# An attention-and-MLP kernel on one Trainium2 core: from blocks of 768 tokens per batch entry to blocks of 384 queries of all heads, each followed by its MLP block

## The chip, the cores and the metric

The kernel runs on one core of one Trainium2 chip. The metric is the device time of one execution in microseconds (us); the kernel before takes 378.56 us (median of three runs, 377.82 to 378.64). Every run has a state, fast or slow, given by its time against the fastest run of the same kernel (over 1.5% longer is slow). Engines are called PE (matrix multiply), PEld (its weight load), DVE (vector), ACT (activations), POOL and SP (here it mainly issues DMA transfers). The "span" of a profile runs from the first to the last instruction of one execution and is about 1.7 us shorter than the time.

## The reference, cut to what matters

q, k and v are [4 batches, 8 heads, 768 tokens, 64], in f32. For each query, an upper bound of its score is worked out for each chunk of 32 keys; the six best chunks that are not in the future are kept, the rest is masked; attention follows, and its output x (3072 tokens of 512 columns) goes through an MLP with an ELU between.

```python
k_min = np.min(k_chunks, axis=3); k_max = np.max(k_chunks, axis=3)
ub = np.sum(np.maximum(q * k_min, q * k_max), axis=-1)        # one bound per query and chunk
top_chunks = np.argsort(np.where(causal, ub, -1e9), axis=-1)[..., -6:]
mask = sel & (pos[:, None] >= pos[None, :])                   # chosen chunk and causal
attn = softmax(np.where(mask, scale * q @ k.T, -1e9))
x = (attn @ v).transpose(0, 2, 1, 3).reshape(B * S, H * D)
h = x @ w_in                                                  # 512 -> 2048
g = np.where(h > 0.0, h, np.exp(np.minimum(h, 0.0)) - 1.0)
return g @ w_out                                              # 2048 -> 512
```

## The kernel before

Two heads make a pair; four pairs make a batch entry, and 16 pairs make the whole. For each pair, `prep` transposes k and q on PE (`psK`, `psQ`, in the PSUM pool psT) and copies them out as bf16 operands of the scores (`lhs`, `rhs`). `select` computes the bounds (`ub`), finds the six best chunks, transposes the resulting mask and sends it by DMA into spare rows of `rhs`, where it enters the scores as extra rows of the contraction. `attend` computes scores (`sps`), exponentials (`pt`) and the attention output, and transposes it on PE into `xt`. `mlp` takes a batch entry and a half of its tokens: PE fills `h_ps`; ACT, POOL and DVE turn it into `gT`, which frees the `h_ps` buffer; PE then fills `o_ps`.

```python
psT = pool("psT", 2, space=bass.MemoryType.PSUM)   # psK, psQ, ub, pxt
psS = pool("psS", 2, space=bass.MemoryType.PSUM)   # sps
psO = pool("psO", 1, space=bass.MemoryType.PSUM)
psM = pool("psM", 3, space=bass.MemoryType.PSUM)   # h_ps, o_ps

    # select(g): the mask goes by one DVE transpose and four DMAs
    selT = selpool.tile([P, NQS], BF16, name="selT")
    nc.vector.transpose(out=selT, in_=sb[:, :, :].rearrange("p b c -> p (b c)"))
    for j in range(2):
        s = (2 * g + j) % NSET
        nc.sync.dma_start(out=rhsA[s][64:64 + NCH, Q0:S], in_=selT[64 * j:64 * j + NCH, :])
        nc.sync.dma_start(out=rhsB[s][0:NCH, Q0:S], in_=selT[64 * j + 32:64 * j + 32 + NCH, :])
    ...
    # mlp(b, hf): one of 16 columns of the hidden layer
    for kk in range(NKK):
        nc.tensor.matmul(hw, lhsT=w_in_sb[:, kk, P * fc:P * (fc + 1)],
                         rhs=xT[NPAIR * b + kk][:, ts], start=(kk == 0), stop=(kk == NKK - 1))
    nc.scalar.activation(out=e_sb, in_=hw, func=AF.Exp)
    nc.gpsimd.tensor_scalar(out=m_sb, in0=e_sb, scalar1=-1.0, scalar2=1.0, op0=AOT.add, op1=AOT.mult)
    nc.vector.scalar_tensor_tensor(out=gT[:, fc, :], in0=hw, scalar=0.0, in1=m_sb,
                                   op0=AOT.max, op1=AOT.min)
    ...
    # the order: attention of all pairs of a batch entry, MLP two groups of pairs later
    for g in range(ng):
        attend(2 * g)
        if g + 1 < ng: select(g + 1)
        attend(2 * g + 1)
        if g + 2 < ng: prep_group(g + 2)
        if g % 2 == 1 and g >= 3:
            for hf in range(2): mlp((g - 3) // 2, hf)
    for hf in range(2): mlp(B - 1, hf)
```

The pools have eight PSUM buffers in all: 2 psT, 2 psS, 1 psO, 3 psM. The program fixes the order of instructions on each engine, with the attention of one batch entry woven into the MLP of another.

The softmax here doesn't subtract the row's maximum and nothing guards it: scores larger than these inputs give would overflow.

Of the kernel before, what the change touches and what calls it, by code (L numbers as in the profile page):

```python
# [9 lines left out]
AOT = mybir.AluOpType  # L10
# [5 lines left out]
B = 4  # L16
# [11 lines left out]
HS = S // 2  # L28
NFC = DFF // P
# [5 lines left out]
NSET = 4  # L35
Q0 = TOPK * CHUNK
NQB = NCH - TOPK
NQS = S - Q0
HB = NQB // 2
HQ = HB * CHUNK  # L40


@with_exitstack
def kernel(
# [17 lines left out]
    smpool = pool("smpool", 3)  # L62
    selpool = pool("selpool", 2)
    ptpool = pool("ptpool", 10)
    opool = pool("opool", 3)
    xtpool = pool("xtpool", 10)
    gtpool = pool("gtpool", 2)
    mlppool = pool("mlppool", 4)
    psT = pool("psT", 2, space=bass.MemoryType.PSUM)
    psS = pool("psS", 2, space=bass.MemoryType.PSUM)  # L70
    psO = pool("psO", 1, space=bass.MemoryType.PSUM)
    psM = pool("psM", 3, space=bass.MemoryType.PSUM)

    npairs = B * NPAIR


    def load(t):
        b, r = divmod(t, NPAIR)
        k_pair = ldpool.tile([P, NQT, 2, D], F32, name="k_pair")
        q_pair = ldpool.tile([P, NQT, 2, D], F32, name="q_pair")  # L80
        for h in range(2):
            nc.sync.dma_start(out=k_pair[:, :, h, :],
                              in_=k[b, 2 * r + h].rearrange("(n p) d -> p n d", p=P))
        for h in range(2):
            nc.sync.dma_start(out=q_pair[:, :, h, :],
                              in_=q[b, 2 * r + h].rearrange("(n p) d -> p n d", p=P))
        return k_pair, q_pair

    def load_v(t):
        b, r = divmod(t, NPAIR)  # L90
        v_pair = ldpool.tile([P, NQT, 2, D], F32, name="v_pair")
        for h in range(2):
            nc.sync.dma_start(out=v_pair[:, :, h, :],
                              in_=v[b, 2 * r + h].rearrange("(n p) d -> p n d", p=P))
        return v_pair

    lds = {t: load(t) for t in range(2)}
    ldv = {t: load_v(t) for t in range(2)}
# [6 lines left out]
    ident_b = const.tile([P, P], BF16, name="ident_b")  # L105
    nc.vector.tensor_copy(out=ident_b, in_=ident_f)

    vexts, lhsA, lhsB, rhsA, rhsB, kst = [], [], [], [], [], []
    for s in range(NSET):
        vexts.append(const.tile([P, NQT, 2, D + 1], BF16, name=f"vext{s}"))  # L110
        lhsA.append(const.tile([P, S], BF16, name=f"lhsA{s}"))
        lhsB.append(const.tile([P, S], BF16, name=f"lhsB{s}"))
        rhsA.append(const.tile([P, S], BF16, name=f"rhsA{s}"))
        rhsB.append(const.tile([P, S], BF16, name=f"rhsB{s}"))
        kst.append(const.tile([P, 2, 64], F32, name=f"kst{s}"))

    def cast_v(t):
        return nc.gpsimd.tensor_scalar(out=vexts[t % NSET][:, :, :, 0:D], in0=ldv.pop(t), scalar1=1.0,
                                       scalar2=0.0, op0=AOT.mult, op1=AOT.add)

    for s in range(NSET):
        nc.vector.memset(kst[s], 0.0)
        nc.vector.memset(vexts[s][:, :, :, D:D + 1], 1.0)
        nc.vector.memset(rhsA[s][64:P, :], 0.0)
        nc.vector.memset(rhsB[s][0:64, :], 0.0)

    econst = const.tile([P, NCH, CHUNK], BF16, name="econst")
    nc.vector.memset(econst, MASKNEG)
    for r0 in (0, 64):
        nc.gpsimd.affine_select(out=econst[r0:r0 + 64], in_=econst[r0:r0 + 64],  # L130
                                compare_op=AOT.is_equal, fill=0.0, base=0,
                                pattern=[[1, NCH], [0, CHUNK]], channel_multiplier=-1)
    for s in range(NSET):
        nc.vector.tensor_copy(out=lhsA[s][64:P, :],
                              in_=econst[64:P].rearrange("p c w -> p (c w)"))
        nc.vector.tensor_copy(out=lhsB[s][0:64, :],
                              in_=econst[0:64].rearrange("p c w -> p (c w)"))

# [4 lines left out]
    selb = [const.tile([P, NQB, CHUNK], BF16, name=f"selb{i}") for i in range(2)]  # L143
    for i in range(2):
        nc.gpsimd.memset(selb[i], 0.0)
# [3 lines left out]

# [8 lines left out]


    qf = {}  # L160

    def prep(t):
        s = t % NSET
        k_pair, q_pair = lds.pop(t)
        kmm = smpool.tile([P, 2, NCH], F32, name="kmm")
        for h in range(2):
            ps = psT.tile([P, HS], F32, name="psK", tag="ps")
            for n in range(3):
                nc.tensor.transpose(ps[:, P * n:P * (n + 1)], k_pair[:, 3 * h + n], ident_f)  # L169
            pv = ps[:, :].rearrange("p (c w) -> p c w", w=CHUNK)  # L170
            cs = slice(12 * h, 12 * h + 12)
            nc.vector.tensor_reduce(out=kmm[:, 0, cs], in_=pv, axis=AX.X, op=AOT.min)  # L172
            nc.vector.tensor_reduce(out=kmm[:, 1, cs], in_=pv, axis=AX.X, op=AOT.max)  # L173
            ts = slice(HS * h, HS * (h + 1))
            nc.scalar.activation(out=lhsA[s][0:64, ts], in_=ps[0:64, :], func=AF.Copy)
            nc.scalar.activation(out=lhsB[s][64:P, ts], in_=ps[64:P, :], func=AF.Copy)  # L176
        for h in range(2):
            rows = slice(64 * h, 64 * h + 64)
            cols = slice(32 * h, 32 * h + NCH)
            nc.gpsimd.tensor_copy(out=kst[s][rows, 0, cols], in_=kmm[rows, 0, :])  # L180
            nc.gpsimd.tensor_tensor(out=kst[s][rows, 1, cols], in0=kmm[rows, 1, :],
                                    in1=kmm[rows, 0, :], op=AOT.subtract)
        QTf = qfpool.tile([P, NQS], F32, name="QTf")
        Qrl = qfpool.tile([P, NQS], F32, name="Qrl")
        qf[t] = (QTf, Qrl)
        for h in range(2):
            ps = psT.tile([P, HS], F32, name="psQ", tag="ps")
            for n in range(3):
                nc.tensor.transpose(ps[:, P * n:P * (n + 1)], q_pair[:, 3 * h + n], ident_f)  # L189
            ts = slice(HS * h, HS * (h + 1))  # L190
            if h == 0:
                nc.scalar.activation(out=QTf[:, 0:HS - Q0], in_=ps[:, Q0:HS], func=AF.Copy)
            else:
                nc.scalar.activation(out=QTf[:, HS - Q0:], in_=ps, func=AF.Copy)  # L194
            nc.scalar.activation(out=rhsA[s][0:64, ts], in_=ps[0:64, :], func=AF.Copy)
            nc.scalar.activation(out=rhsB[s][64:P, ts], in_=ps[64:P, :], func=AF.Copy)  # L196
        nc.vector.tensor_scalar(out=Qrl, in0=QTf, scalar1=0.0, scalar2=None, op0=AOT.max)  # L197


    def select(g):  # L200
        ubT = selpool.tile([P, NQB, CHUNK], F32, name="ubT")
        for u in range(2):
            ub = psT.tile([P, HQ], F32, name="ub", tag="ps")
            for w in range(2):
                for j in range(2):
                    t = 2 * g + j
                    nc.tensor.matmul(ub[64 * j:64 * j + 64, :], lhsT=kst[t % NSET][:, w, :],  # L207
                                     rhs=qf[t][w][:, HQ * u:HQ * (u + 1)],
                                     start=(w == 0), stop=(w == 1))
            nc.vector.transpose(out=ubT[:, HB * u:HB * (u + 1), :].rearrange("p b c -> p (b c)"),  # L210
                                in_=ub)
        nc.vector.memset(ubT[:, 0, TOPK + 1:TOPK + 2], -BIG)
        thr8 = selpool.tile([P, NQB, 8], F32, name="thr8")
        for bb in range(NQB):
            nc.vector.max(out=thr8[:, bb, :], in_=ubT[:, bb, 0:max(8, bb + TOPK + 1)])
        sb = selb[g % 2]
        nc.vector.tensor_tensor(out=sb[:, :, 0:NCH], in0=ubT[:, :, 0:NCH],
                                in1=thr8[:, :, TOPK - 1:TOPK].to_broadcast([P, NQB, NCH]),
                                op=AOT.is_lt)
        selT = selpool.tile([P, NQS], BF16, name="selT")  # L220
        nc.vector.transpose(out=selT, in_=sb[:, :, :].rearrange("p b c -> p (b c)"))
        for j in range(2):
            s = (2 * g + j) % NSET
            nc.sync.dma_start(out=rhsA[s][64:64 + NCH, Q0:S], in_=selT[64 * j:64 * j + NCH, :])
            nc.sync.dma_start(out=rhsB[s][0:NCH, Q0:S], in_=selT[64 * j + 32:64 * j + 32 + NCH, :])
# [6 lines left out]

    def attend(t):
        s = t % NSET
        lhs = (lhsA[s], lhsB[s])
        rhs = (rhsA[s], rhsB[s])
        xt = xtpool.tile([P, S], BF16, name="xt")
        xT[t] = xt
        for grp in range(2):
            seg = {}  # L240
            for segs in steps[grp]:
# [3 lines left out]
                for hd in range(2):  # L245
                    if not (both and hd == 1):
                        sps = psS.tile([P, 512], F32, name="sps")
# [142 lines left out]
```

## Time and profile before

| stage of the profiled run | length, us | PE busy, us | PE clock | DMA share |
|---|---|---|---|---|
| start, loads and first heads | 36 | 17.7 | 0.89 | 0.88 |
| heads, no MLP result yet | 49 | 38.5 | 0.73 | 0.97 |
| attention and MLP mixed | 205 | 186.0 | 0.98 | 0.22 |
| MLP alone | 88.3 | 76.5 | 1.00 | 0.09 |

The table is the view by windows of the kernel before, whose rows follow. Its columns are the window, its length, busy time of each engine (with the number of instructions), then the granted PE clock as a share of full speed, the busy share of the DMA engines, and GB/s.

```profile
core 0: us, PE busy (x) PEld busy (x) DVE busy (x) ACT busy (x) POOL busy (x), PEclk, DMA share, GB/s
0.00:36.00 36.00, 17.71 (x65) 10.55 (x66) 20.67 (x68) 17.02 (x37) 12.67 (x35) 0.89 0.88 183
36.00:85.00 49.00, 38.47 (x301) 21.85 (x300) 24.55 (x92) 34.20 (x72) 8.81 (x17) 0.73 0.97 186
85.00:290.00 205.00, 186.01 (x1487) 106.04 (x1495) 125.11 (x371) 147.46 (x329) 56.15 (x127) 0.98 0.22 57
290.00:378.30 88.30, 76.53 (x412) 38.17 (x414) 34.98 (x64) 26.75 (x54) 25.70 (x50) 1.00 0.09 37
```

Busy time of PE is not work: at half clock an instruction is busy for longer and does the same. In one run three transposes of k take 0.90 us at clock 0.50 and 0.49 at full clock. So the page's engine line and its slices are read together. One caution: in this trace the view by windows gives a clock of 1.00 for the first 24 us, yet three transposes of q take 0.90 us there (at 13.14 us), so the 0.89 of the first stage says too much. The slices cut the span into 40 parts of 9.5 us; a digit is tenths busy (9 is 90% or more), and the clock is in tenths of full speed.

```profile
PE 318.7 (84%) x2260; PEld 176.6 (47%) x2272; DVE 205.3 (54%) x594; ACT 225.4 (60%) x489; POOL 103.3 (27%) x228
...
PE   1476876889599999599997799999999989979886
...
PEclk9995697589989999989998999999999999999999
DMA  9949999935914526501000000102000100101002
```

PE is busy 84% of the time, but the fourth to the ninth digit of its clock line (28 to 85 us) lie between 5 and 9 tenths, and the DMA line stands at 9 in seven of the first eight slices. The view of waits (who waited, for what; us in total, times, longest) has PE's largest total wait, which lies within the MLP:

```profile
PE h_ps L302 <- DVE gT L310: 12.8, 24, 2.4
```

The timeline of ACT, kernel before, gives the moment of the first MLP result, when the first `h_ps` is evicted (read out of its buffer). Columns: start, length, engine and line, instruction with its count, and in brackets the idle time just before it with what ended it.

```profile
85.56 1.25 ACT L306 ACTIVATE e_sb<-h_ps 128x384 f32<-128x384 f32 x3
```

The same kind of view, the timeline, of PE in the kernel before shows the tail:

```profile
328.69 2.11 PE L302 MATMUL h_ps<-xt,w_in_sb 128*128 128x384 bf16 x12 [0.53 <-DVE gT L310]
331.32 2.12 PE L302 MATMUL h_ps<-xt,w_in_sb 128*128 128x384 bf16 x12 [0.52 <-DVE gT L310]
```

The first `h_ps` is evicted (read out of its buffer) at 85.56 us, since an MLP block waits for four whole pairs. PE's first MLP matmul is much earlier, as the view of the tile `h_ps` up to 90 us shows (count, shortest/median/longest in ns, first and last start):

```profile
L302 PE MATMUL h_ps<-xt,w_in_sb x19: 323/325/527, 43.5 to 89.8; 128*128 128x384 bf16 x19
```

It starts at 43.5 us with the first pair's share of the sum and then waits for the other pairs.

In the tail, three `h_ps` buffers let 12 matmuls pass (2.11 us), then PE stands for 0.52 us until `gT` frees one.

Two lines from the chain that ended last (start, length, what) show what holds the first heads: a load of k, and a mask on its way by DMA.

```profile
36.67 9.29 DMA k_pair<-in_k_dram
...
53.91 4.36 DMA rhsA_137<-selT
```

### The profile page before, as it was taken

To read this page: it belongs to the slowest core of one execution; us is meant where nothing else is said; L and a number is where in the kernel's file an instruction comes from. 1 tells how busy PE (TensorE), PEld (TensorE's weight loads), DVE (VectorE), ACT (ScalarE), POOL (GpSimd) and SP (SyncE) were. 2 spreads that over 40 slices of the span, in tenths; PEclk is the share of its full clock that TensorE was granted. 3 is DMA by queue.
4 is the path that set the end of the run, shared out by engine and by line. 5 is a ranking of instruction groups with operands and counts; after the bars stand their busy time and mean duration, and the time that the engine had idled before them with its cause. 6 is when DMAs were issued, how large, how long until landed. Compare 5 with 4: busy or idle time off the path is not lost.

```text
span 378.3 us, 6504 instructions
## 1 busy us (share of the span) xinstructions
PE 318.7 (84%) x2260; PEld 176.6 (47%) x2272; DVE 205.3 (54%) x594; ACT 225.4 (60%) x489; POOL 103.3 (27%) x228
## 2 busy tenths in 40 slices
PE   1476876889599999599997799999999989979886
PEld 1333444455265455354564454545556444444442
DVE  7553275367477475561694683651867154261540
ACT  1638757858968965950879758653797052350430
POOL 4414022003133112340331231430123053250430
PEclk9995697589989999989998999999999999999999
DMA  9949999935914526501000000102000100101002
GB/s 205 277 74 192 203 181 177 280 71 118 209 42 98 125 71 161 117 2 55 30 12 2 1 14 28 58 0 83 5 11 2 57 29 26 58 3 55 28 2 83
DMA packets 84129, 30.67 MB, mean 81 GB/s; under 512 B 76160, under 2 KB 81024, under 8 KB 84096
## 3 DMA queue, kind: packets, MB, share of 16 engines
q1 hardware_dynamic: 79872, 26.06, 27.7%
q0 software_dynamic: 4224, 4.19, 7.1%
q8 instruction: 18, 0.29, 0.3%
q14 instruction: 15, 0.12, 0.1%
HBM read 27.26 MB, written 6.29 MB: 89 GB/s over the span
## 4 chain that ended last, share of the span: by engine, by line
PE 27%; issue 23%; ACT 21%; POOL 12%; DVE 11%; DMA 4%; POOLq 0%; SPq 0%; ACTq 0%; DVEq 0%
POOL m_sb L308 12%; PE o_ps L315 8%; ACT pt L253 6%; PE sps L250 4%; PE ub L207 4%; PE h_ps L302 4%; DMA k_pair<-in_k_dram 2%; DVE gT L310 2%; PE psQ L189 2%; ACT e_sb L306 2%; ACT QTf L194 1%; PE psK L169 1%; DMA rhsA_137<-selT 1%; ACT pt L256 1%; PE pxt L291 1%
## 5 line engine op out<-in xcount | busy, mean ns | idle before, releaser
L302 PE MATMUL h_ps<-xt,w_in_sb 128*128 128x384 bf16 x512 | 108.4, 333 | 13.2 <-DVE gT L310 12.8
L308 POOL TENSOR_SCALAR m_sb<-e_sb 128x384 f32<-128x384 f32 x128 | 65.9, 518 | 179.0 <-ACT e_sb L306 162.3
L253 ACT ACTIVATE pt<-sps 128x384 bf16<-128x384 f32 (+1 forms) x160 | 80.1, 536 | 37.2 <-PE sps L250 35.9
L310 DVE SCALAR_TENSOR_TENSOR gT<-h_ps,m_sb 128x384 bf16<-128x384 f32 x128 | 70.0, 554 | 43.7 <-POOL m_sb L308 40.4
L315 PE MATMUL o_ps<-w_out_sb,gT 128*128 128x512 bf16 x372 | 87.4, 379 | 0.6
L306 ACT ACTIVATE e_sb<-h_ps 128x384 f32<-128x384 f32 x128 | 62.3, 495 | 39.1 <-PE h_ps L302 37.8
L302 PEld LDWEIGHTS <-w_in_sb 128*128 128x128 bf16 x512 | 49.1, 99 | 49.1 <-issue 22.7
L315 PEld LDWEIGHTS <-gT 128*128 128x128 bf16 x384 | 36.9, 98 | 40.1 <-issue 1.0
L321 DVE COPY o_sb<-o_ps 128x512 f32<-128x512 f32 x16 | 11.0, 690 | 50.8 <-PE o_ps L315 50.8
L280 PEld LDWEIGHTS <-pt 128*128 128x128 bf16 x672 | 29.3, 102 | 16.4 <-DVE pt L262 6.4
L189 PE MATMUL psQ<-ident_f,q_pair 128*128 128x128 f32 x96 | 21.6, 345 | 17.8 <-ACT lhsB_124 L176 7.9
L319 ACT ACTIVATE o_sb<-o_ps 128x512 f32<-128x512 f32 x8 | 4.8, 597 | 39.5 <-PE o_ps L315 39.4
L169 PE MATMUL psK<-ident_f,k_pair 128*128 128x128 f32 x96 | 19.6, 323 | 8.7 <-DMA k_pair<-in_k_dram 4.3
L189 PEld LDWEIGHTS psQ<-ident_f,q_pair 128*128 128x128 f32 x96 | 12.4, 168 | 29.3 <-ACT lhsB_124 L176 10.5
L262 DVE TENSOR_TENSOR pt<-pt,tri_174 128x512 bf16<-128x512 bf16 x32 | 14.3, 446 | 12.8 <-ACT pt L253 12.6
L256 ACT ACTIVATE pt<-sps 128x512 bf16<-128x512 f32 x32 | 19.6, 611 | 1.4 <-PE sps L250 1.3
L197 DVE TENSOR_SCALAR Qrl<-QTf 128x576 f32<-128x576 f32 x16 | 7.4, 462 | 23.8 <-ACT QTf L194 23.8
L172 DVE TENSOR_REDUCE kmm<-psK 128x12 f32<-128x384 f32 x32 | 17.7, 552 | 4.2 <-PE psK L169 3.5
L169 PEld LDWEIGHTS psK<-ident_f,k_pair 128*128 128x128 f32 x96 | 11.9, 160 | 17.3 <-ACT rhsB_126 L196 5.3
L173 DVE TENSOR_REDUCE kmm<-psK 128x12 f32<-128x384 f32 x32 | 17.4, 545 | 0.0
L292 DVE COPY xt<-pxt 128x384 bf16<-128x384 bf16 x32 | 11.3, 353 | 11.2 <-PE pxt L291 10.7
L250 PE MATMUL sps<-rhsA_125,lhsA_123 128*128 128x384 bf16 (+2 forms) x36 | 10.3, 325 | 4.4 <-ACT pt L253 4.2
(220 smaller groups left out, 404.2 us busy)
## 6 DMA issues: line engine op xcount, KB each, us to landing
k_pair<-in_k_dram SPq DMA_DIRECT2D x32, 192.0 KB
q_pair<-in_q_dram SPq DMA_DIRECT2D x32, 192.0 KB
v_pair<-in_v_dram SPq DMA_DIRECT2D x32, 192.0 KB
out_dram<-o_sb SPq DMA_DIRECT2D x24, 256.0 KB
w_in_sb<-in_moe_w_in_dram POOLq DMA_DIRECT2D x4, 512.0 KB, 7.0
w_out_sb<-in_moe_w_out_dram POOLq DMA_DIRECT2D x4, 512.0 KB, 8.0
rhsA_125<-selT SPq DMA_DIRECT2D x4, 27.0 KB
rhsB_126<-selT SPq DMA_DIRECT2D x4, 27.0 KB
```

Source lines behind the costliest of these rows:

```text
L169: nc.tensor.transpose(ps[:, P * n:P * (n + 1)], k_pair[:, 3 * h + n], ident_f)
L172: nc.vector.tensor_reduce(out=kmm[:, 0, cs], in_=pv, axis=AX.X, op=AOT.min)
L189: nc.tensor.transpose(ps[:, P * n:P * (n + 1)], q_pair[:, 3 * h + n], ident_f)
L250: nc.tensor.matmul(sps[:, o + pc:o + pc + w], lhsT=lhs[hd][:, P * kb:P * (kb + 1)], rhs=rhs[hd][:, c0:c0 + w], start=True, stop=True)
L253: nc.scalar.activation(out=pt[:, hd, 0:wtot], in_=sps[:, 0:wtot], func=AF.Exp, scale=SCALE)
L256: nc.scalar.activation(out=pt[:, :, 0:256], in_=sps[:, :].rearrange("p (h w) -> p h w", h=2), func=AF.Exp, scale=SCALE)
L280: nc.tensor.matmul(o3[:, hd, qi, :], lhsT=pt[:, hd, P * qt + off:P * qt + off + P], rhs=vexts[s][:, kb, hd, :], start=(kb == 0), stop=(kb ...
L302: nc.tensor.matmul(hw, lhsT=w_in_sb[:, kk, P * fc:P * (fc + 1)], rhs=xT[NPAIR * b + kk][:, ts], start=(kk == 0), stop=(kk == NKK - 1))
L306: nc.scalar.activation(out=e_sb, in_=hw, func=AF.Exp)
L308: nc.gpsimd.tensor_scalar(out=m_sb, in0=e_sb, scalar1=-1.0, scalar2=1.0, op0=AOT.add, op1=AOT.mult)
L310: nc.vector.scalar_tensor_tensor(out=gT[:, fc, :], in0=hw, scalar=0.0, in1=m_sb, op0=AOT.max, op1=AOT.min)
L315: nc.tensor.matmul(o_ps, lhsT=gT[:, fc, P * tt:P * (tt + 1)], rhs=w_out_sb[:, fc, :], start=(fc == 0), stop=(fc == NFC - 1))
```

## The change

The change has several parts. Its intent is to begin the MLP earlier and to leave less of it alone at the end. The block becomes 384 queries of all eight heads of a batch entry (eight blocks in all); the MLP of a block runs beside the attention of the next. All else serves this: loads of 384 tokens; operands kept for eight pairs; one score operand of 96 rows per head (64 rows of k or q, 32 of mask), so the mask can be written in place by DVE transposes of 32 rows rather than by DMA; the x of six of the eight blocks transposed by DMA rather than by PE; psT cut to one buffer and psM raised to four; several small operations moved among DVE, POOL and ACT. The diff is shortened; `...` marks what is left out.

```diff
-psT = pool("psT", 2, ...)          psM = pool("psM", 3, ...)
+psT = pool("psT", 1, ...)          psM = pool("psM", 4, ...)
+PE_T = (0, 7)                      # blocks whose x is transposed by PE
 ...
-        k_pair = ldpool.tile([P, NQT, 2, D], F32, name="k_pair")      # 768 tokens, 2 heads
+        xp = ldpool.tile([P, 3, 2, D], F32, name=name)                # 384 tokens, 2 heads
         for h in range(2):
+            (eng or nc.sync).dma_start(out=xp[:, :, h, :],
+                 in_=x[b, 2 * r + h, HS * hf:HS * (hf + 1)].rearrange("(n p) d -> p n d", p=P))
 ...
-        selT = selpool.tile([P, NQS], BF16, name="selT")
-        nc.vector.transpose(out=selT, in_=sb[:, :, :].rearrange("p b c -> p (b c)"))
         for j in range(2):
             s = (2 * g + j) % NSET
-            nc.sync.dma_start(out=rhsA[s][64:64 + NCH, Q0:S], in_=selT[64 * j:64 * j + NCH, :])
-            nc.sync.dma_start(out=rhsB[s][0:NCH, Q0:S], in_=selT[64 * j + 32:64 * j + 32 + NCH, :])
+            for h in range(2):
+                r0 = 64 * h + 32 * j
+                nc.vector.transpose(out=rhs[s][h][64:96, qlo:qhi],
+                                    in_=sb[r0:r0 + 32].rearrange("p b c -> p (b c)"))
 ...
+        if via_pe: ...      # as before: three PE transposes, one DVE copy
+        nc.sync.dma_start_transpose(out=xt[:, :].rearrange("p (n t) -> p n t", n=3),
+                                    in_=on[:, :, :, :].rearrange("p q h d -> p (q h d)"))
 ...
+    for t in pairs_of(0): load_v(t, 0)
+    front(0)                                # prep and select of block 0
+    casts = vpart(0)                        # POOL: v of block 0 to bf16
+    with tc.issue_after(casts[1].ins):      # the weights, on POOL's DMA queue
+        load_w_in(0); load_w_in(1)
+    with tc.issue_after(casts[3].ins):
+        load_w_in(2); load_w_in(3)
+        for i in range(4): load_w_out(i)
+    for i in range(len(blocks)):
+        for t in pairs_of(blocks[i][0]): attend(t, blocks[i][1], i in PE_T)
+        if i + 1 < len(blocks):
+            for t in pairs_of(b1): load_v(t, hf1)
+            front(i + 1)
+        if i >= 1: mlp(*blocks[i - 1])
+        if i + 1 < len(blocks): vpart(i + 1)
+    mlp(*blocks[-1])
```

## The prediction

> **What bounds it now.** PE is busy 318.7 of 378.3 us (engine table), but not at its pace throughout. The windows view gives four stages:
> - 0 to 36 us: PE 17.7 busy; DMA share 0.88.
> - 36 to 85: PE 38.5, granted clock only 0.73, DMA share 0.97. The chain of waits shows 9.3 us for one k load. The first h_ps eviction comes at 85.6 us: an MLP block needs four whole 768-query head pairs.
> - 85 to 290: mixed; PE 186 of 205, ACT 147.
> - 290 to 378: MLP alone. Three h_ps buffers let 12 matmuls (2.11 us) pass, then PE waits 0.52 us for gT.
>
> [...] this trace shows 0.50 at 30 to 40 us, where PE was 66% busy.
>
> **PE floor, estimated from full-clock durations in the trace.** h_ps 512 x 0.176 = 90; o_ps 384 x 0.218 = 84; k and q transposes 192 x 0.183 = 35; bounds (ub) 8 x 2.1 = 17; scores about 36; attention times v about 27; x transposes about 6. Sum about 295 us, so about 83 us are start, slow clock, stalls and tail.
>
> **What the change moves.**
> - Half-size blocks: the first MLP block needs 1.6 MB of q and k, not 3.1. I expect first MLP matmuls at 40 to 50 us. This is the main gain: 25 to 35 us less lost at the start.
> - Only the last half-block's MLP is left alone (about 25 us, not 88). Four h_ps buffers remove most of the 0.52 us stalls: 2 to 3 us per block.
> - x by DMA in 6 of 8 blocks: PE loses 72 transposes (about 4.5 us), DVE 24 copies (8.5 us). The latency hides behind a block of other work.
> - Masks: per two pairs one 0.77-us DVE transpose and four DMAs go; eight 32-row transposes come, about 3.3 us: DVE +20 us in total. kst on DVE, about +8; output copies to ACT, DVE -11, ACT +9.6; initial fills leave DVE, about -5. DVE stays about 205, ACT rises to about 235.
> - Scores with 96 rows for 128: same columns streamed, no gain. Bounds in 32-column strips: four together where two were, half the steps over twice the columns: no change if the strips overlap.
> - A single psT buffer is a loss: transposes, bounds and their evictions serialise (about 2 us per tile, some 20 us per block of about 38), seen as PE waits for ACT or DVE at psK and psQ.
>
> **Sum.** About 30 us of unproductive start (was about 45, with slow clock), middle at some 88% of PE's pace (was 82%), tail about 27: **340 us**, range **320 to 366**. Faster by over 2%: 0.90; within 2%: 0.06; slower: 0.04.
>
> **What would show it.** Right: first evicted h_ps before 55 us; granted clock back at 1.0 by 60 us; MLP alone at the end under 32 us; ACT 230 to 240 us; DVE 200 to 212; h_ps waits for gT under 0.2 us; no PE wait for xt's DMA.
>
> **What would make it wrong.** (1) ACT: in second-half blocks prep and exp take about 30 us of ACT beside 10 of MLP, against about 38 us of PE. If MLP isn't interleaved finely, ACT stalls PE and we land above 355. (2) Single psT serialising prep. (3) DMA transposes holding up the SP queue or the engines[...]. (4) Weights late, so MLP starts at 60. (5) Better: a middle at 95% of the floor gives about 318.

Two of its statements can be read off the two traces. A score matmul of 384 columns takes 0.32 us at full clock with 128 rows (before) and with 96 (after). The strips of the bounds do overlap: before, two start within 0.01 us of each other (at 214.93 and 214.94 us, 0.46 us each), after, four within 0.02 (93.70 to 93.72, 0.35 us each). Its 2 us per psT tile, 3.3 us for eight mask transposes, and 30 and 10 us of ACT against 38 of PE are estimates of mine that name no measured number.

## The result, and the profile after

The changed kernel takes 356.81 us (median of four fast runs, 355.8 to 359.6), against 378.25 us for the kernel before in the same rounds. The ratio is 0.9445, with a 95% interval of 0.939 to 0.950. Ratios here are the mean time of one kernel's fast runs over the mean of the other's fast runs of the same rounds, so they are not quite the ratio of the medians quoted. On the four chips used for the experiments the kernel before took 381.0 to 381.5 us; an unedited copy of the changed kernel took 355.91 us on one of them (ratio 0.9345), so the gain is 21 to 26 us.

The first view is again the view by windows, of the kernel after, in the columns described above.

```profile
0.00:30.00 30.00, 18.65 (x131) 11.32 (x132) 22.24 (x77) 16.55 (x34) 19.31 (x63) 0.74 1.00 187
30.00:50.00 20.00, 6.69 (x39) 3.67 (x38) 4.47 (x13) 3.94 (x9) 3.16 (x7) 0.67 1.10 200
50.00:70.00 20.00, 16.10 (x84) 8.10 (x83) 14.92 (x46) 12.30 (x27) 9.86 (x20) 0.78 0.62 140
70.00:85.00 15.00, 14.39 (x137) 7.75 (x135) 10.30 (x35) 13.13 (x30) 3.00 (x6) 1.00 0.45 100
85.00:320.00 235.00, 218.08 (x1787) 118.80 (x1786) 158.66 (x503) 170.81 (x385) 53.87 (x107) 1.00 0.28 71
320.00:354.80 34.80, 31.18 (x161) 15.47 (x158) 10.21 (x20) 11.91 (x23) 8.76 (x18) 1.00 0.12 46
```

The next lines are the engine line and the slices of its page (8.9 us each).

```profile
PE 305.1 (86%) x2328; PEld 165.1 (47%) x2328; DVE 220.8 (62%) x690; ACT 228.6 (64%) x506; POOL 98.0 (28%) x219
...
PE   4577149799987899998998799998998899999995
...
PEclk9855858899999999999999999999999999999999
DMA  7999976644654333251424223222321001000102
```

The middle and the tail have become nearly full: PE is busy 218 of 235 us at full clock between 85 and 320. The start has not. From 30 to 50 us PE is busy 6.7 of 20 us at a clock of 0.67, with the DMA engines full (share 1.10; since it passes one, packet times must overlap). The timeline of all engines, kernel after, from 32 to 49 us shows how it looks from within (SPq is SP's DMA queue):

```profile
32.37 3.80 PE L310 MATMUL h_ps<-xt,w_in_sb 128*128 128x384 bf16 x15
...
34.85 0.49 ACT L313 ACTIVATE e_sb<-h_ps 128x384 f32<-128x384 f32 x1 [5.70 <-PE h_ps L310]
...
36.19 8.98 SPq L83 DMA_DIRECT2D v_pair<-in_v_dram  x8
...
44.73 0.51 POOL L159 TENSOR_SCALAR vext_129<-v_pair 128x384 bf16<-128x384 f32 x1 [22.11 <-DMA v_pair<-in_v_dram]
...
47.67 0.51 POOL L314 TENSOR_SCALAR e_sb<-e_sb 128x384 f32<-128x384 f32 x1
48.22 0.56 DVE L316 SCALAR_TENSOR_TENSOR gT<-h_ps,e_sb 128x384 bf16<-128x384 f32 x1 [14.07 <-POOL e_sb L314]
48.83 1.44 PE L310 MATMUL h_ps<-xt,w_in_sb 128*128 128x384 bf16 x4 [11.85 <-DVE gT L316]
```

PE starts on the MLP at 32.37 us (before: 43.5), and the first result is taken up at 34.85, where before it was 85.56. PE fills its four `h_ps` buffers and stops. At 47.67 POOL works on `e_sb`, which ACT had ready at 35.3: POOL takes its instructions in the order of the program, and the cast of the next block's v stood ahead and waited 22.11 us for its data. So DVE waits 14.07 us for POOL, and PE 11.85 us for DVE. The SP queue shows why v is late: its issue of eight v loads took 8.98 us, from 36.19 on.

The DMA view of the first 50 us of the kernel after lists packets, megabytes and the share of the 16 engines' time for each queue, then the issues with KB each and median us from issue to landing:

```profile
DMA packets 26110, 9.61 MB, mean 192 GB/s; under 512 B 22011, under 2 KB 26107, under 8 KB 26107
...
q1 hardware_dynamic: 20283, 4.99, 50.3%
q0 software_dynamic: 4224, 4.19, 50.1%
...
w_in_sb<-in_moe_w_in_dram POOLq DMA_DIRECT2D x4, 512.0 KB, 9.9
w_out_sb<-in_moe_w_out_dram POOLq DMA_DIRECT2D x4, 512.0 KB, 20.2
```

Half of all DMA time goes to q, k and v (q1, packets of 256 bytes; ACT's queue carries another 1,600 of them), and half to the weights (q0). Two estimates follow from these lines. Sixteen engines for 50 us are 800 us of DMA time; 50.3% of it over 20,283 packets is 19.8 ns per packet, and the q, k and v of two blocks (4.72 MB, 18,432 packets) therefore take 22.9 us of all engines. The weights take 50.1% of 50 us, 25 us. Together that is 48 us of DMA time: by this estimate nearly all that the DMA engines do in the first 50 us is what two blocks and the MLP must have. It is not quite all: ten loads of the third block (96 KB each) are issued in this window too. The weights weigh double: 4.19 MB is what is written as bf16, while the page's line of bytes read from HBM, 27.26 MB, is only reached with both weights counted as 8.39 MB of f32.

The transfers that SP issues and those that POOL issues share the DMA engines' time: 50.3% and 50.1% of the 16 engines over these 50 us. Counted from the trace's packets in steps of 4 us, from 16 to 40 us the weights take 0.91 to 0.93 of the engines' time and q, k and v 0.3 beside them.

The tail of the kernel after, on PE's timeline:

```profile
319.90 10.52 PE L321 MATMUL o_ps<-w_out_sb,gT 128*128 128x512 bf16 x48
330.26 10.56 PE L310 MATMUL h_ps<-xt,w_in_sb 128*128 128x384 bf16 x64
340.66 10.52 PE L321 MATMUL o_ps<-w_out_sb,gT 128*128 128x512 bf16 x48
```

Sixty-four matmuls of `h_ps` run without a pause; before, each dozen was followed by 0.52 us. PE's MLP runs alone from 319.90 to 351.2 us.

### Where the time went: work done by a given moment

Because neither busy time nor waits add up to the change, I count work: every PE instruction in a window is counted at its full-clock length, read from this trace (`h_ps` 0.176 us, `o_ps` 0.219, a k or q transpose 0.183, an x transpose 0.11, three in 0.33, attention times v 0.036, the bounds 2.09 per 16 of 288 columns, a score by its columns: starts lie 0.11 us apart for 256 and 0.16 for 384). It is an estimate from one profiled run of each kernel, good to 1 or 2 us at a window's edge, and records missing from a trace count as lost time: the trace of before lacks 12 of its 384 `o_ps` matmuls, 2.6 us. Cumulated us of PE work:

| work done by, us | 50 | 85 | 140 | 200 | 290 | 320 | end |
|---|---|---|---|---|---|---|---|
| before | 19 | 39 | 84 | 138 | 220 | 248 | 297 (378.3) |
| after | 16 | 43 | 92 | 148 | 230 | 259 | 292 (354.8) |
| e9_quarter_w | 26 | 57 | 105 | 160 | 244 | 274 | 292 (340.6) |
| e5_psT2 | 16 | 38 | 83 | 139 | 217 | 245 | 291 (372.4) |
| e6_mask_dma_r2 | 11 | 41 | 84 | 135 | 215 | 242 | 289 (370.5) |
| e10_order_r2 | 16 | 39 | 88 | 142 | 219 | 245 | 290 (368.5) |
| e7_before_psM4 | 13 | 34 | 76 | 132 | 219 | 250 | 298 (369.7) |
| e12_order_psM | 21 | 51 | 101 | 152 | 232 | 261 | 289 (350.7) |

Time minus work is loss. Before: 46 us up to 85, 24 from 85 to 290, 11 in the tail. After: 42 up to 85, 19 from 85 to 320, 2 in the tail. The span is 23.5 us shorter: about 4 us from the start, 5 from the middle, 9 from the tail, and 5 from less work (the x transposes that PE no longer does, 72 x 0.11 = 8 us, less the missing records). The start was to bring 15; that is the shortfall that the experiments look into. No run changes the size of the blocks alone, so these shares are read from the count and not shown by an experiment.

### The profile page after: what moved, and what is told of

It reads as the page before. It is cut to its first block, busy times and chain, and to the rows that moved or that the text cites. A ratio compares the mean times of both kernels' runs of the same rounds, so it can differ in the third digit from the quotient of the medians.

```text
span 354.8 us, 6831 instructions
## 1 busy us (share of the span) xinstructions
PE 305.1 (86%) x2328; PEld 165.1 (47%) x2328; DVE 220.8 (62%) x690; ACT 228.6 (64%) x506; POOL 98.0 (28%) x219
## 3 DMA queue, kind: packets, MB, share of 16 engines
q0 software_dynamic: 4224, 4.19, 7.1%
HBM read 27.26 MB, written 6.29 MB: 95 GB/s over the span
## 4 chain that ended last, share of the span: by engine, by line
PE 33%; ACT 16%; DVE 8%; issue 2%; POOL 1%; ACTq 0%; POOLq 0%
PE o_ps L321 18%; PE h_ps L310 7%; ACT pt L257 6%; ACT e_sb L313 3%; PE sps L254 3%; DVE gT L316 2%; PE ub L214 2%; ACT pt L260 2%; PE psK L173 1%; POOL e_sb L314 1%; PE psQ L192 1%; ACT QTf L193 1%; DVE kmm L175 1%; ACT o_sb L324 1%; DVE on L290 1%
## 5 line engine op out<-in xcount | busy, mean ns | idle before, releaser
L310 PE MATMUL h_ps<-xt,w_in_sb 128*128 128x384 bf16 x512 | 113.5, 336 | 17.2 <-DVE gT L316 17.0
L314 POOL TENSOR_SCALAR e_sb<-e_sb 128x384 f32<-128x384 f32 x128 | 65.1, 516 | 190.9 <-ACT e_sb L313 158.3
L316 DVE SCALAR_TENSOR_TENSOR gT<-h_ps,e_sb 128x384 bf16<-128x384 f32 x128 | 69.1, 550 | 52.2 <-POOL e_sb L314 50.4
L321 PE MATMUL o_ps<-w_out_sb,gT 128*128 128x512 bf16 x384 | 90.1, 379 | 0.0
L257 ACT ACTIVATE pt<-sps 128x384 bf16<-128x384 f32 (+1 forms) x160 | 80.1, 547 | 11.4 <-PE sps L254 10.5
L324 ACT ACTIVATE o_sb<-o_ps 128x512 f32<-128x512 f32 x24 | 14.3, 597 | 53.8 <-PE o_ps L321 50.0
L266 DVE TENSOR_TENSOR pt<-pt,tri_196 128x512 bf16<-128x512 bf16 x32 | 13.5, 421 | 12.8 <-ACT pt L257 12.6
L192 PE MATMUL psQ<-ident_f,q_pair 128*128 128x128 f32 x96 | 18.2, 295 | 3.7 <-ACT lhs_167 L178 0.8
L193 ACT ACTIVATE QTf<-psQ 128x192 f32<-128x192 f32 (+1 forms) x32 | 13.4, 418 | 8.3 <-PE psQ L192 7.9
L196 DVE TENSOR_SCALAR Qrl<-QTf 128x192 f32<-128x192 f32 (+1 forms) x32 | 10.3, 323 | 11.7 <-ACT QTf L193 11.1
L217 DVE STREAM_TRANSPOSE ubT<-ub 128x192 f32<-128x192 f32 (+1 forms) x16 | 7.6, 478 | 10.1 <-PE ub L214 10.1
L272 DVE TENSOR_TENSOR pt<-pt,tri_196 128x256 bf16<-128x256 bf16 x32 | 9.8, 306 | 4.6 <-ACT pt L260 3.8
```

The costliest lines, as they stand in the source:

```text
L192: nc.tensor.transpose(ps[:, P * n:P * (n + 1)], q_pair[:, n], ident_f)
L257: nc.scalar.activation(out=pt[:, hd, 0:wtot], in_=sps[:, 0:wtot], func=AF.Exp, scale=SCALE)
L314: nc.gpsimd.tensor_scalar(out=e_sb, in0=e_sb, scalar1=-1.0, scalar2=1.0, op0=AOT.add, op1=AOT.mult)
L321: nc.tensor.matmul(o_ps, lhsT=gT[:, fc, P * tt:P * (tt + 1)], rhs=w_out_sb[:, fc, :], start=(fc == 0), stop=(fc == NFC - 1))
L324: nc.scalar.activation(out=o_sb, in_=o_ps, func=AF.Copy)
```

## The experiments

Theory A: POOL's order alone holds the start; the `e_sb` work is ready and stands behind casts of v that wait for a late load. Move the v and the stall goes, 10 us or so. Theory B: DMA binds the first 50 us; moving one load ahead of others only moves the wait to another instruction, and only less DMA work helps. Separately, some of the other parts of the change are undone one at a time. A variant, A', is that whatever stands ahead of `e_sb` in POOL's queue holds it, the issue of a transfer as well as a cast. Experiments of one job ran on one chip and share the runs of before. A suffix _r2 marks a second entry: the first reached no chip, through no fault of the kernel. All kernels give correct results except e9_quarter_w.

One thing decides how far each run can be read. An edit can also change the order of PE's instructions in the whole program. Compared by kind of matmul, in order of start, the traces of e1, e3, e8 and e9 keep the order of the changed kernel (98% or more of the sequence matches). Those of e2, e4, e5, e6, e10 and e12 match in only 34 to 63%, and that of e7 matches the kernel before in 62%. So the first group isolates its edit; the second measures the edit together with another order.

### Control: the changed kernel, unedited (after_again)

> The changed kernel unedited, as the control of this chip: 0.9445 of the time before, as on record (0.939 to 0.95).

Measured: 355.91 us (355.59 to 356.96), ratio 0.9345 (0.9316 to 0.9373). PE waits for `gT` 18.0 us in all, longest 12.2. This is what the runs below are held against; by ratio where the chip differs.

### The next block's v loaded early (e1_v1_early)

```diff
-        xp = ldpool.tile([P, 3, 2, D], F32, name=name)
+        xp = ldpool.tile([P, 3, 2, D], F32, name=name, bufs=8 if name == "v_pair" else 4)
 for t in pairs_of(0): load_v(t, 0)
+for t in pairs_of(0): load_v(t, 1)       # and not again inside the loop for i == 0
```

> Edit: the value loads of block 1 are issued right after those of block 0, ahead of block 1's keys and queries (eight v buffers instead of four). Theory A: the 11.85 us in which PE waits for gT at 37 us comes from POOL, whose in-order queue holds the cast of block 1's values (which waits for a late load) ahead of the first MLP block's e_sb. Then the wait shrinks to under 2 us and the time falls by 9 to 15 us, to 342 to 348. Rival B: the start is bound by the bytes to be moved (DMA share 1.2 there), so the wait only moves to block 1's k and q (PE waits of 5 us or more at psK or psQ) and the time changes by less than 3 us.

Measured: 356.03 us (355.28 to 358.92), ratio 0.9361: no gain. PE's waits in the first 80 us of this kernel:

```profile
PE psK L173 <- DMA k_pair<-in_k_dram: 20.1, 3, 15.2
...
PE h_ps L310 <- DVE gT L316: 0.9, 2, 0.8
```

The wait for `gT` is gone (0.9 us), and one of 15.2 us for a k load stands in its place. This speaks against A and for B.

### The next block's v by a casting DMA, no cast on POOL (e3_v1_cast_dma)

```diff
+                for h in range(2):      # block 1 only; its four casts on POOL go
+                    nc.gpsimd.dma_start(out=vexts[t % NSET][:, 3:6, h, 0:D],
+                                        in_=v[b1, 2 * (t % NPAIR) + h, HS:S].rearrange("(n p) d -> p n d", p=P))
```

> Edit: block 1's values go by a casting DMA from POOL's queue straight into vext, so POOL has no cast to wait with; the bytes and the other loads stay. Theory A: no instruction of POOL waits for a value load before the first e_sb, so the 11.85 us wait of PE goes although the values land no earlier than before (44 us or later); time 342 to 350. Rival B: no gain, the wait reappears at the loads. Rival A': the DMA issues queue in POOL behind the weights and hold POOL as the cast did; then POOL shows the wait at the issue and the time stays at 355 to 358.

Measured: 357.2 us (356.0 to 358.1), ratio 0.9375: no gain. The casts are gone, but POOL now waits to issue these transfers behind the weights on its own queue (10.3 us for w_out, 6.4 for w_in), and PE still waits 12.1 us for `gT` in the first 85 us (two waits, the longer 8.1). The POOL queue holds `e_sb` in either form; once more a wait has moved.

### w_out loaded later (e2_wout_late)

```diff
-        for i in range(4):
-            load_w_out(i)
...
+            later = vpart(i + 1)
+            if i == 0:
+                with tc.issue_after(later[3].ins):
+                    for w in range(4): load_w_out(w)
```

> Edit: the four w_out loads are issued after the casts of block 1's values instead of after block 0's. Load order of q, k, v as in the changed kernel. Theory A (POOL's queue holds a cast that waits for a load slowed by the weights): block 1's first value tile arrives about 10 us earlier (35 us instead of 44.7), the h_ps wait falls from 11.9 to under 4 us, time 344 to 350. Rival B (bytes in all bind the start): w_out then arrives late, PE waits for it at o_ps by 5 us or more, time within 3 us of 356.8.

Measured: 372.72 us in the median, 367.15 and 371.0 in the two fast runs (two were slow, among them the profiled one), ratio 0.9689: 13 us more than the control by ratio. In the profile POOL's casts still wait for v (longest 15.6 us), DVE waits 14.4 us for POOL, and PE 11.3 us behind DVE. The profile is of a slow run, so I take no more from it than that the stall did not go. Neither theory expected a loss of 13 us, and where it comes from is not known, so this run decides nothing between A and B.

### A quarter of the weights loaded, used four times (e9_quarter_w; wrong result)

```diff
-                nc.tensor.matmul(hw, lhsT=w_in_sb[:, kk, P * fc:P * (fc + 1)],
+                nc.tensor.matmul(hw, lhsT=w_in_sb[:, kk, P * (fc % 4):P * (fc % 4 + 1)],
-                ... rhs=w_out_sb[:, fc, :],
+                ... rhs=w_out_sb[:, fc % 4, :],
-        load_w_in(1)
-        load_w_in(2); load_w_in(3)
-        for i in range(4): load_w_out(i)
+        load_w_out(0)
```

> Wrong result on purpose. Edit: only one quarter of w_in and of w_out is loaded and used four times over; every instruction of the five engines stays, only six of the eight weight loads go (3/4 of about 27 us of all DMA engines). Theory B: the values of block 1 land some 15 to 20 us earlier than 44.7, the 11.85 us wait of PE for gT goes and the clock comes back earlier; time 335 to 343. Theory A with bytes unimportant: the POOL wait stays and the time falls by less than 3 us.

Measured: 341.9 us (341.3 to 342.3), ratio 0.8967 against the control's 0.9345 on the same chip: 14 us less, with the same compute instructions. The windows view of 32 to 50 us, of the control (window, length, busy PE, PEld, DVE, ACT, POOL, clock, DMA share, GB/s):

```profile
32.00:50.00 18.00, 5.80 (x22) 2.97 (x20) 2.21 (x6) 4.05 (x9) 2.52 (x5) 0.59 1.07 197
```

The same window of e9_quarter_w:

```profile
32.00:50.00 18.00, 15.10 (x90) 7.77 (x90) 13.46 (x41) 11.82 (x27) 10.29 (x21) 0.93 0.61 138
```

PE's busy time in this window rises from 5.8 to 15.1 us and its clock from 0.59 to 0.93, with the DMA share down to 0.61. PE still waits for `gT`, but at most 1.1 us at a time. So it is the DMA work of the first 50 us that binds, as B says (bytes or number of packets, this run can't tell); the estimate of 25 us for all weights (q0 has 7.1% of the span in both traces: 25.2 us after, 26.9 before) would make the three quarters that are missing 19 us, of which 14 showed. The run gives the size of the limit, not a remedy: a right result needs all of the weights.

### Larger packets for k and q (e8_kq_768)

```diff
-  .rearrange("(n p) d -> p n d", p=P)            # k and q
+  .rearrange("(p n) d -> p n d", p=P)            # three tokens in a row per partition
-            nc.tensor.transpose(ps[:, P * n:P * (n + 1)], k_pair[:, n], ident_f)
+            nc.tensor.transpose(ps[:, :].rearrange("p (t n) -> p n t", n=3)[:, n, :], k_pair[:, n], ident_f)
```

> Edit: keys and queries are loaded with three consecutive tokens per partition (768 contiguous bytes in the source instead of 256; the transposes write every third column, which restores the order). The bytes are the same. Theory B (the start ends when the DMA engines have moved the q, k, v of blocks 0 and 1 and both weight matrices: 18,400 packets of 256 bytes at about 20 ns and 4,096 of the weights at about 95 ns on 16 engines, 49 us): [...] If the packets stay at 256 bytes because of the destination's layout, nothing changes (within 2 us of the control) and the run says nothing about B. Theory A (POOL's order alone) expects no change.

Measured: 361.24 us (358.4 to 363.5), ratio 0.9476, some 5 us slower than the control. The packets did not grow: I counted 18,102 packets for 4.45 MB in the first 50 us, 246 bytes each (the changed kernel's q1: 20,283 for 4.99 MB, also 246). The tile keeps the two heads side by side, so its rows are still broken at every 64 elements, 256 bytes; that this is the reason is my guess, as a tile with the heads apart was not run. So the test says nothing about B; it shows only that this edit is no gain, and why it costs 5 us was not looked into. Whether larger packets would help stays open.

### An order made to fit the arrival (e10_order_r2)

```diff
+            if i == 0: (v of block 1 loaded just behind its k and q)
-    with tc.issue_after(casts[1].ins):      # weights behind block 0's casts
+    casts1 = vpart(1)
+    with tc.issue_after(casts1[1].ins):     # weights behind block 1's casts
+        if i == 1:
+            with tc.issue_after(gate[0]):   # mlp(0) on PE behind attention of block 1's second pair
+                mlp(*blocks[0])
+            with tc.issue_after(last_e[0]): # later casts of v behind the ninth e_sb
+                vpart(i + 1)
```

> Edit: the same work and bytes, in an order that fits when the loads can land: block 1's v loads directly behind its k and q; both weight matrices behind the casts of block 1's v; the first MLP block's matmuls behind the attention of block 1's second pair on PE; on POOL each block's v casts behind the ninth e_sb of the MLP block issued alongside. Theory B' (the start moves 9.6 MB in 50 us whatever the order, but the order decides what PE can do meanwhile): by 50 us PE has done about 25 us of work (counted at full-clock durations) instead of 16, no PE wait over 5 us before 85 us except the first load, the clock is back at 1.0 before 40 us; time 338 to 348 against 355.9 of the control. If instead the loss at the start is bytes alone, the weights now land later and PE waits for w_in by as much as was gained: 353 us or more.

Measured: 368.26 us (367.6 to 370.2), ratio 0.9676: 13 us more than the control by ratio. The timeline of PE in this kernel:

```profile
36.23 0.90 PE L192 MATMUL psQ<-ident_f,q_pair 128*128 128x128 f32 x3 [2.19 <-ACT lhs L178]
38.64 0.90 PE L173 MATMUL psK<-ident_f,k_pair 128*128 128x128 f32 x3 [1.51 <-ACT rhs L195]
```

With no MLP beside it, the preparation of block 1 runs through one psT buffer: PE does 0.9 us of transposes, then waits 1.5 to 2.2 us for ACT to copy them out. Its clock is 0.50 in the window of 32 to 50 us, with PE busy for 6.89 of the 18 us and no idle stretch longer than 2.2; what sets the clock is not shown. This is the loss that the prediction feared of the single psT; in the changed kernel the MLP can fill such gaps, because w_in has come by then. It is only a part of the 13 us, though: by the table this kernel is 4 us behind the changed one at 85 us and 11 at 290, and the later part is not explained. The expected 338 to 348 us failed: by 50 us PE had done 16 us of work and not 25.

In the changed kernel, for comparison, the clock is not steadily full until about 70 us of 354.8, and the mean over the span is 0.947 in the profiled run.

### The same order, with block 1 prepared in psM (e12_order_psM)

```diff
-        pool0 = (psM, "psm") if (t < NPAIR and hf == 0) else (psT, "ps")
+        pool0 = (psM, "psm") if t < NPAIR else (psT, "ps")      # and the same in select
+ own v buffers for block 1; first part of w_in behind block 0's casts; later casts behind the sixth e_sb
```

> Follows the run with the new order, which lost (368 us) because PE, with no MLP work to fill in, walked block 1's preparation through the single psT buffer: 33 to 62 us, 2.4 to 3 us per tile at half clock. Edit to that run: block 1's transposes and bounds use the four MLP buffers, as block 0's do; the first quarter of w_in goes behind block 0's casts (the DMA share was 0.76 up to 32 us); v of block 1 has its own four buffers; later casts stand behind the sixth e_sb. If the single psT was what the new order lost to, the wait chain psQ, lhs, psK, rhs between 33 and 62 us goes, PE has done 24 us of work or more by 50 us (the control 16, the run before 15.5) and the time is 340 to 350. If ACT binds block 1's attention there (29 us of it), PE still idles at sps and the time is 350 to 357. At 357 or more the order theory is wrong.

Measured: 352.37, 359.86, 356.55 and 358.35 us (the second and fourth count as slow), ratio 0.9387 (0.9337 to 0.9438) against the control's 0.9345 on another chip. No gain is shown, although the profiled run, at 350.7 us of span, was the shortest of any correct kernel here. Two rows of its windows view, in the columns as before:

```profile
32.00:50.00 18.00, 14.26 (x75) 6.57 (x74) 13.56 (x51) 13.38 (x30) 2.98 (x5) 0.79 1.22 200
50.00:70.00 20.00, 17.83 (x207) 10.92 (x206) 13.73 (x49) 18.35 (x43) 3.10 (x7) 1.00 0.79 161
```

The start is better: by 85 us PE has done 51 us of work, the changed kernel 43. It loads the same bytes, so on this one profile, that of its fastest run, Theory B is too narrow in saying that only less DMA work helps: the order decides what PE can do meanwhile. But the lead is 2 us at 290, in the table above. After 85 us PE waits 5.3 us for ACT at `psK` and 2.1 at `psQ`, the single psT again (the control 1.0 and 1.9); the rest I could not place.

### Two psT and three psM buffers (e5_psT2)

```diff
-psT = pool("psT", 1, ...)   psM = pool("psM", 4, ...)
+psT = pool("psT", 2, ...)   psM = pool("psM", 3, ...)
```

> Edit: the PSUM split of the kernel before inside the changed one: two psT buffers, three MLP buffers. The MLP-only end (one h_ps phase) loses about 3 us to 0.52 us waits; if a single psT costs little (PE waits at psK and psQ sum to about 4 us after 70 us), the total is 3 to 8 us slower than the control; if the single psT is what keeps the middle at 91% of PE's pace, this run is faster than the control by 3 us or more.

Measured: 374.08 us (372.9 to 375.0), ratio 0.9815: 18 us slower than the control on the same chip, most of the gain. By the table it is 5 us of work behind at 85, 13 at 290. PE's waits for `gT` are 14.1 us here, about as much in total as in the control (18.0), but spread (19 waits). So the direct waits do not account for 18 us. The order of instructions is built with the pools in view and changes with them, so this run measures the split of buffers together with the order that comes of it.

### The kernel before with one psT and four psM buffers (e7_before_psM4)

```diff
-psT = pool("psT", 2, ...)   psM = pool("psM", 3, ...)
+psT = pool("psT", 1, ...)   psM = pool("psM", 4, ...)
```

> The kernel before with only the PSUM split of the change: one psT buffer instead of two, four MLP buffers instead of three. In the MLP-only end the 0.52 us waits of PE for gT go (about 4 per block and 4 blocks: 8 to 10 us less). The single psT buffer costs in the first 85 us, where preparation binds: if that is as large as the prediction feared (2 us per tile not hidden), the start gets 10 us or more longer and the total is 376 to 390; if scheduling hides it, the total is 368 to 372.

Measured: 373.19 us (371.42 to 374.38), ratio 0.9807 (0.976 to 0.9855): about 7 us come from this edit, 5 to 9 by the interval, with the order of instructions that it brings. From the view of waits, PE in this kernel over the whole span:

```profile
PE psK L169 <- ACT lhsB L176: 11.4, 7, 4.8
...
PE h_ps L302 <- DVE gT L310: 4.5, 7, 1.6
```

The waits for `gT` fall from 12.8 to 4.5 us, and waits at the one psT appear: 11.4 us at `psK`. They fall in the start, where this kernel, too, has no MLP to put between (34 us of work by 85, before 39); the later stages pay that back.

### x by PE in all blocks (e4_x_pe_r2)

```diff
-PE_T = (0, 7)
+PE_T = tuple(range(8))
```

> Edit: x is transposed by PE in all eight blocks, no DMA transposes. The prediction gave the DMA transposes a gain of about 4.5 us of PE (72 transposes; measured in the old trace: 0.11 us each, about 8 us) and 8.5 us of DVE. If both lie on the critical path the run is 5 to 10 us slower than the control (361 to 366), and more if the one psT buffer makes them queue; if PE's middle has slack for them, within 2 us.

Measured: 363.5 and 364.1 us in the fast runs (two others slow, 370 and 373, the profiled one among them), ratio 0.9555: 8 us more than the control by ratio (0.021 of 381). The length of the 72 transposes that return to PE is 72 x 0.11 = 8 us, which agrees; with two fast runs the interval (0.947 to 0.964) allows 5 to 11 us, and the order of PE's instructions changed too (52% matches), so the agreement is no proof. In the changed kernel a DMA transpose of x lands 2.3 us after issue (a k load of 96 KB 2.5, both medians of its page), and no wait of PE for it is in the view of waits. Its issue takes longer: 1.2 us on SP, against 0.48 for a load (at 85.04 us).

### Masks by DMA, as before (e6_mask_dma_r2)

```diff
+        selT = selpool.tile([P, HS], BF16, name="selT")
+        nc.vector.transpose(out=selT[:, 0:nq], in_=sb[:, :, :].rearrange("p b c -> p (b c)"))
-                nc.vector.transpose(out=rhs[s][h][64:96, qlo:qhi], in_=sb[r0:r0 + 32]...)
+                nc.sync.dma_start(out=rhs[s][h][64:96, qlo:qhi], in_=selT[r0:r0 + 32, 0:nq])
```

> Edit: the masks reach the 96-row tiles as before, one 128-row DVE transpose and four small DMAs per two pairs and half, instead of four 32-row DVE transposes. DVE gets about 22 us less busy (30 us of 32-row transposes against 8). If DVE isn't on the critical path, the gain of the change here is only the shorter latency of the mask (0.4 to 0.6 us against 2 to 4 us through a DMA): 0 to 5 us slower than the control; if DVE's load matters, 2 to 6 us faster.

Measured: 372.35 us (369.9 to 373.3), ratio 0.9771: 16 us more than the control by ratio. The longest wait of PE, from the view of waits of this kernel, lies in the start:

```profile
PE sps L255 <- DMA rhs<-selT: 18.3, 1, 18.3
```

The timeline of the SP queue of the same kernel shows what stood ahead (start, length of issue, transfers):

```profile
22.27 4.80 SPq L83 DMA_DIRECT2D q_pair<-in_q_dram  x2
27.16 5.54 SPq L83 DMA_DIRECT2D k_pair<-in_k_dram  x2
32.80 4.80 SPq L83 DMA_DIRECT2D q_pair<-in_q_dram  x2
37.70 7.10 SPq L233 DMA_DIRECT2D rhs<-selT  x8
```

The mask transfers stand in the SP queue behind loads whose issue takes long while the DMA engines are full (9 tenths or more from 9 to 37 us in the page's slices), and scores wait 18.3 us for them. The transfer itself is short: a mask lands 1.8 us after its issue, in the median over the whole run. The transpose that fills `selT` had ended at 22.0 us; the transfers are issued from 37.7 on. The k and q loads just ahead took 4.8 to 5.5 us of issue per two; at 50.30 us, in the same queue, two took 0.96. By 50 us this kernel had done 11 us of work, the changed one 16. Yet this wait isn't most of the 16 us: the changed kernel has its own wait of 11.85 us for `gT` in the same stretch, and by 85 us e6 is only 2 us behind (41 against 43), at 290 15 (215 against 230). So most of the loss arises after 85 us. In this later part the clock was 0.94 from 85 to 200 us (1.00 in the changed kernel), and up to 320 us PE waits 6.7 us for ACT's `pt` and 7.8 for `gT` (1.3 and 4.4 in the changed kernel). Why the middle got worse is not shown; the order of PE's instructions changed with the edit (50% of the sequence matches).

## Why the prediction was right or wrong

The predicted 340 us was 17 us too low; the measured 356.81 lies in the range of 320 to 366, and the direction was right.

- **The step that failed, its size and not its direction: "Half-size blocks ... first MLP matmuls at 40 to 50 us. This is the main gain: 25 to 35 us less lost at the start"**. My sum then used less, "about 30 us of unproductive start (was about 45)", so the prediction did not even agree with itself. The first MLP matmul came even sooner, at 32 us, and the loss up to 85 us fell only from 46 to 42. That is 12 us of the 17. I took an early first matmul for an early steady pace, though the kernel before had its first at 43.5 us, inside the 40 to 50 that I predicted for the change. What was left out is the sum of the DMA work: two blocks of q, k and v with both weights fill the DMA engines for 48 us (estimate above). In the kernel before the first `h_ps` was finished at 85 us, so w_out was not needed until then. e9_quarter_w shows it: with fewer weight bytes and the same instructions, 14 us come back. e1 and e3 show that moving a load or a cast moved the wait and gained nothing, so POOL's order alone is not the cause; e12 shows that a different order can win 8 us by 85 us, though it lost most of them later. Point (4) of what would make it wrong named late weights, but gave no cost.
- **The clock.** Predicted full by 60 us; it was steadily full by 70 (the window of 50 to 70 us has 0.78). The evictions of `h_ps` before 55 us held, at 34.85.
- **The middle** was put at 88% of PE's pace, from 82%. By the count of work it is 92% (216 of 235 us), and before it was 88% (181 of 205): the gain was about right, the level too low. At 88% the 216 us of work would have taken 245 us. The prediction's own terms (290 us of work, 30 lost at the start, 28 in a middle of 235 us at 88%, 2 in the tail) come to some 350 us, not 340. So the parts don't add up to its number, and the error of the middle hides a part of that of the start: that the range held is in part luck.
- **The tail held.** Predicted about 27 us, under 32; PE ran the MLP alone for 31.3 us. Waits for `gT` of 0.52 us are gone there.
- **The four psM buffers** had no term of their own in the sum, only "2 to 3 us per block". Alone, in the kernel before, they gave 7 us net of the single psT (with another order). Undone in the changed kernel, they cost 18 us, more than the waits for `gT` that the profile of before shows in all (12.8). Why so much is not settled.
- **The single psT** was feared as a chain of some 20 us per block. Where the MLP fills the gaps it costs little: after 70 us of the changed kernel no wait of PE at `psK` or `psQ` is longer than 0.8 us. The fear was right where nothing fills them (e10_order_r2, and the start of e7_before_psM4).
- **x by DMA** was put at "about 4.5 us" of PE; it is 72 x 0.11 = 8 us, and about 8 us (5 to 11) were measured. The term "x transposes about 6" for 96 of them should have been 10.6. There is no wait of PE for it, as predicted.
- **The masks** were counted only as a DVE cost of 20 us. The trace has +24: eight transposes, 3.76 us per two pairs, against one of 0.77. But DVE is busy for only 62% of the span, and with the masks back on DMA the kernel is 16 us slower (e6), with some 22 us less DVE work. Of these 16 us the wait behind loads in the SP queue explains a few; the rest is open. The line of 4.36 us for such a transfer in the chain of before was in the profile, and I did not use it.
- **DVE 200 to 212 and ACT 230 to 240** were missed: 220.8 and 228.6. On DVE the masks (+24), the `kst` and `kmm` work (+13, put at 8) and the `Qrl` clamp (+3) were larger, the copies removed (8.5 and 11.0) as expected. In the chain that ended last of the changed kernel PE has 33% of the span, ACT 16% and DVE 8%: both are on that chain, with smaller shares.

These lines show the mask transposes on DVE, in the view by groups (count, busy us, mean ns). First the kernel before:

```profile
L221 DVE STREAM_TRANSPOSE selT<-selb_177 128x576 bf16<-128x576 bf16 x4 | 3.1, 767 | 0.0
```

Then the kernel after, one group for 384 and one for 192 columns:

```profile
L231 DVE STREAM_TRANSPOSE rhs_151<-selb_204 32x384 bf16<-32x384 bf16 x2 | 1.1, 574 | 0.0
...
L231 DVE STREAM_TRANSPOSE rhs_139<-selb_199 32x192 bf16<-32x192 bf16 x2 | 0.7, 374 | 0.1
```

The cost goes with the columns, not with the rows: 32 rows of 384 columns take 0.57 us, and so do the 128 rows of 384 columns of the bounds' transpose (0.577 us in the kernel after, in f32); 576 columns take 0.77.

What stays open: why e5_psT2 loses as much as 18 us, e6_mask_dma_r2 16 and e2_wout_late and e10_order_r2 13; where e12_order_psM gives back its lead; and whether larger packets would shorten the start. The three parts undone one at a time (e4, e5, e6) cost 8, 18 and 16 us, 42 in all, of a gain of 21 to 26. So they are not shares of the gain. In each of them PE's order changed as well, and by the table e5, e6 and e10 lose more after 85 us than before it. The order is a rival cause for all of these sizes, which no run separates from the edit. No version was shown to beat the changed kernel.

## What to carry to other kernels

When a change makes an engine start earlier, add up the bytes that must land by then, at the rates of the trace, since an early first matmul says nothing about the second dozen. Moving one load about within a window where DMA was full only renamed the wait here (e1, e3). A single PSUM buffer was cheap where independent work lay between its uses (waits of at most 0.8 us) and dear where none did (11.4 us in the start of e7), so judge it by what the order puts there. Look at what stands ahead of a small transfer that gates compute: here masks waited 15.7 us in a queue behind bulk loads. And when an edit undoes one part, count the work by stage, and check that the order of instructions stayed, before naming the cause: the longest wait of e6 lay in the start, most of its loss did not.
